# One decode step of an adaLN block: a row of w2 loaded in two parts over different DMA engines, five filler products fewer, one row of products cut finer

## The chip, the cores and the metric

The kernel runs on one core of one Trainium2 chip. The metric is the device time of one execution in microseconds (us); less is better. The core has five engines with queues of their own: PE (TensorE, matrix products), DVE (VectorE), ACT (ScalarE), POOL (GpSimd) and SP (SyncE, which here only issues loads). Sixteen DMA engines move the data between memory and the chip; one load is cut into shares that some or all of the sixteen carry, each engine working off its own list in order.

## The reference

Two tokens (B = 2, one position each, D = 512) pass through an attention block over a window of cached keys and values and then a feed-forward block, both with scales, shifts and gates computed from a condition `c`:

```
mod = silu(c) @ w_mod                              # six vectors of 512: sa, ca, ga, sb, cb, gb
h = layernorm(x) * (1 + ca) + sa
q = h @ wq                                         # 32 heads of 128
p = softmax(q . k / sqrt(128)) over the last 4096 of 32768 keys; o = p . v   # 8 kv heads
x = x + ga * (o @ wo)                              # wo: 4096 x 512
h = layernorm(x) * (1 + cb) + sb
x = x + gb * (silu(h @ w1) @ w2)                   # w1: 512 x 1792, w2: 1792 x 512
```

All is float32. The weights and the cache windows are 97.5 MB, and each byte is used for two tokens only.

## The kernel before, in words

All large inputs are loaded by SP, in the order in which they are used, into a ring of eight slots of 16 KB for each partition (`stream`, `load_group`, `load_runs`): w_mod, wq, then keys and values of four groups in turn, then wo, w1 and w2. A load waits on SP until its slot's last reader, on PE, is done. PE works off the products in the order of the program (`inorder`). A float32 product of the program stands in the profile as two records.

The end of the kernel is what the change touches. In the order of PE's queue:

- `busy(4)`: four filler products into a bank that nobody reads (`junk`, line 387). Each is a product of a 128x32 identity with a 128x512 tile of zeros.
- `acc_o` (line 417): 32 products with wo, four at a time in the four column groups of PE.
- `gather` (lines 396 to 410): ACT copies `acc_o` out of PSUM in two halves, and four small products (`ao`, line 404) add the four column groups up. Ahead of these four stands one filler product (`fill=1`), behind them another (`busy(1)`).
- DVE forms the new x and its column sums; `mean_b` (line 446) is a small product for the mean, and `busy(1)` follows it.
- `hid` (line 459): 16 products with w1, with the small product `var_b` (line 468) in the middle, and `busy(2)` behind them.
- DVE and ACT: transpose (`hidT`), scale (`z`), silu, to `uT` (line 487).
- w2 is 14 rows of 128 partitions x 512 numbers (`w2t[0]` to `w2t[13]`), in five loads: rows 0 to 7, rows 8 to 10, and rows 11, 12 and 13 alone. Rows 0 to 10 are the wide products `acc_yw` (line 491): row tt goes to column group tt % 4. ACT copies `acc_yw` to `y_sb` in two halves (line 513).
- `turned_products` (line 503): rows 11, 12 and 13 are multiplied the other way round, with the weights of w2 as the stationary side and two columns of `uT` moving. Between them the two halves of `y_sb` are turned and added in the same bank, `yx`. Row 11 goes in calls of 64 columns (`m=64`), the others in calls of 32.
- One scan on DVE (line 524) applies the gate, and ACT issues the store.

The host hands w2 over in another order of its columns, and takes the answer out of the stored tile.

Of the kernel before, what the change touches and what calls it, by code (L numbers as in the profile page):

```python
# [13 lines left out]
P = 128  # L14
B, D = 2, 512
HQ, HKV, DH = 32, 8, 128
G = HQ // HKV
F = 1792
# [5 lines left out]
def adaln_block(  # L24
# [21 lines left out]
    nc = tc.nc  # L46
# [12 lines left out]
    def const(shape, name):  # L59
        return consts.tile(shape, F32, name=name)  # L60

    def bank(tag, name):
        return (psum1 if tag in "CO" else psum).tile([P, 512], F32, tag=tag, name=name)
# [4 lines left out]
    def stream(n=1):  # L68
        i = turn_of[0]
        if n % 4 == 0:  # L70
            i += -i % n
        turn_of[0] = i + n
        return slots[:, i % RING : i % RING + n, :].rearrange("p s e -> p (s e)")
# [7 lines left out]
    def load_runs(w, per, lo, hi):  # L81

        e = w.shape[1]
        n = -(-(hi - lo) * e // 4096)
        t = stream(n)[:, : (hi - lo) * e].rearrange("p (q e) -> p q e", e=e)
        nc.sync.dma_start(t, w.rearrange("(p q) e -> p q e", q=per)[:, lo:hi, :])
        return t
# [104 lines left out]
    for k in range(4):  # L192
        ab = wm[:, k, : 2 * D].rearrange("p (s g m) -> p g s m", s=2, g=4)
        cd = wm[:, k, 2 * D :].rearrange("p (s g m) -> p g s m", s=4, g=4)
        for g in range(4):
            r = slice(32 * g, 32 * g + 32)
            nc.tensor.matmul(m_a[r, :], scT[:, k, :], ab[:, g], start=(k == 0), stop=(k == 3))  # L197
        for g in range(4):
            r = slice(32 * g, 32 * g + 32)
# [19 lines left out]
    hT, uT = const([P, 4, 32], "hT_b"), const([P, F // P, 32], "uT")  # L219
# [9 lines left out]
    for n in range(2):  # L229
        q_ps = bank("D", f"q{n}")  # L230
        for k in range(4):
            for g in range(4):
                lo = (16 * n + 4 * g) * DH
# [4 lines left out]
                    start=(k == 0),  # L238
                    stop=(k == 3),
# [3 lines left out]
        for g in range(G):  # L243
# [4 lines left out]
                start=True,  # L248
                stop=True,
            ))  # L250
        for b in range(B):
            for s in range(2):
                lo = 256 * (2 * b + n) + 48 * s
# [124 lines left out]
    for lo, hi in ((0, 3), (3, 4)):  # L378
        wt = load_runs(w1, 4, lo, hi)
# [4 lines left out]
    def busy(n):  # L384

        for _ in range(n):
            inorder(nc.tensor.matmul(  # L387
                junk[0:32, :],
                id4,
                warm,  # L390
                start=True,
                stop=True,
            ))


    def gather(acc, wide, name, start, stop, fill=0):

        sb_ = once.tile([P, D], F32, tag="wide", name=name)
        for c in (slice(0, D // 2), slice(D // 2, D)):
            inorder(nc.scalar.copy(sb_[:, c], wide[:, c]))  # L400
        if fill:
            busy(fill)
        for g in range(4):
            inorder(nc.tensor.matmul(
                acc[32 * g : 32 * g + 32, :],
                id4,
                sb_[:, g * P : (g + 1) * P],
                start=start,
                stop=stop,
            ))  # L410

    acc = bank("D", "acc_o")
    ao = bank("A", "ao")[:, :P]
    busy(4)
    for q in range(32):
# [5 lines left out]
            start=(q < 4),  # L421
            stop=(q >= 28),
        ))
    gather(ao, acc, "acc_o_sb", True, True, fill=1)
    busy(1)
    T2, WIDE = F // P, 11
    w2t = {}
    for lo, hi in ((0, 8), (8, 11), (11, 12), (12, 13), (13, T2)):
        wt = load_runs(w2, T2, lo, hi)
        for tt in range(lo, hi):  # L430
            w2t[tt] = wt[:, tt - lo, :]
    aoT = once.tile([P, 4, 32], F32, tag="zp", name="aoT")
# [11 lines left out]
    nc.vector.tensor_reduce(ks, x1T.rearrange("p k b -> p b k"), axis=AX.X, op=ALU.add)  # L444
    mean = bank("B", "mean_b")
    inorder(nc.tensor.matmul(mean[:, :B], mean512, ks, start=True, stop=True))
    busy(1)
    dT = once.tile([P, 4, B], F32, tag="dT", name="dT")
    nc.vector.tensor_sub(dT, x1T, mean[:, None, :B].to_broadcast([P, 4, B]))
    nc.vector.tensor_mul(hT[:, :, 0:32:16], dT, cbT[:, :, 0:32:16])  # L450
# [6 lines left out]
    for k in range(4):  # L457
        for g in range(4):
# [4 lines left out]
                start=(k == 0),  # L463
                stop=(k == 3),
            ))
        if k == 1:
# [3 lines left out]
            nc.scalar.activation(std, var[:, :B], AF.Sqrt, bias=eps_t)  # L470
            rstd = once.tile([P, B], F32, tag="rstdb", name="rstd_b")
            nc.vector.reciprocal(rstd, std)
    busy(2)
    hidT = once.tile([P, T2, 32], F32, tag="pr", name="hidT")
    nc.vector.transpose(hidT, hp.rearrange("p (m t) -> p t m", t=T2))
    z = once.tile([P, T2, B], F32, tag="z", name="z")
# [12 lines left out]
    for tt in range(WIDE):  # L489
# [5 lines left out]
            start=(tt < 4),  # L495
            stop=(tt >= WIDE - 4),
        ))

    def turned_products(rows, u, ks=range(4), start=False, stop=False, m=32):

        for k in ks:
            for g in range(0, P, m):
                inorder(nc.tensor.matmul(  # L503
                    yT[g : g + m, k, :, 0],
                    rows[:, k * P + g : k * P + g + m],
                    u,
                    start=start and k == 0,
                    stop=stop and k == 3,
                ))
# [2 lines left out]
    for c in (slice(0, D // 2), slice(D // 2, D)):  # L512
        inorder(nc.scalar.copy(y_sb[:, c], yw[:, c]))
    for h, tt in enumerate(range(WIDE, T2)):
        turned_products(
            w2t[tt],
            uT[:, tt, 0:32:16],
            start=(h == 0),
            stop=(tt == T2 - 1),
            m=32 if h else 64,  # L520
        )
        if h < 2:
            turned_products(y_sb, id4[:, 0:32:16], range(2 * h, 2 * h + 2))
    inorder(nc.vector.tensor_tensor_scan(yo, g0, yx, 0.0, op0=ALU.mult, op1=ALU.add))  # L524
# [48 lines left out]
```

## Time and profile before

| | |
|---|---|
| median of 3 runs | 233.94 us (233.76 to 233.95) |
| profiled execution | 233.89 us, of which 232.3 us are the profile's span |
| busy share of the span | PE 54%, weight loads 18%, DVE 9%, ACT 7%, POOL 2% |
| DMA | 97.66 MB at 420 GB/s over the span; 97.6% of the sixteen engines' time |
| mean granted clock of PE | 0.801 of full |

The profile covers one execution, from the first instruction to the end of the store. Rows of its views give the start, the time, the engine, the line of the program, the operation and the tiles (written <- read), with what ended the idle time before it in square brackets. PEld is the loading of a product's stationary side, which runs beside the products. The granted clock is what share of full speed the chip let PE run at; it is 1.00 or 0.50 in each stretch. The time of a product in the records holds its way through the array, so that products in a row overlap.

### The profile page before, as it was taken

The page shows a single profiled execution, that of the slowest core. Times are in us where ns is not written, and L with a number is a line of the kernel's source. Part 1 is how long each engine was busy: PE and PEld are TensorE (multiplying, and loading weights), DVE is VectorE, ACT ScalarE, POOL GpSimd, SP SyncE. Part 2 cuts the span into 40 slices and gives each one's busy share as a digit, 9 for nine tenths or more (in the row PEclk, how much of TensorE's full clock was granted, in tenths as well). Part 3 has the DMA queues.
Part 4 walks back from the last instruction along what each step waited for, and adds up shares of the span by engine and source line. Part 5 has one row for each costly group of instructions (what it writes and reads, how often), then busy time and mean ns, then how long its engine had stood idle before and what let it go on. Part 6 is the DMA issues. An engine that isn't in the chain of part 4 may idle for free.

```text
span 232.3 us, 2204 instructions
## 1 busy us (share of the span) xinstructions
PE 125.5 (54%) x976; PEld 42.4 (18%) x976; DVE 21.9 (9%) x74; ACT 17.3 (7%) x39; POOL 5.2 (2%) x22
## 2 busy tenths in 40 slices
PE   0004905840950781495096068139509506999877
PEld 0001401320210221121033012112202102232223
DVE  0005330110021000003000001200000210000230
ACT  2000210000012010001001000100100100000331
POOL 4003010000000000000000000000000000000000
PEclk9999995985796596578579659957857965999999
DMA  7999898998989989899899999999999999999993
GB/s 271 432 495 429 372 530 361 508 398 361 530 372 508 395 364 519 384 496 398 374 496 406 496 395 386 474 418 474 406 395 465 429 446 406 432 392 444 414 410 133
DMA packets 2916, 97.66 MB, mean 420 GB/s; under 512 B 460, under 2 KB 476, under 8 KB 1116
## 3 DMA queue, kind: packets, MB, share of 16 engines
q1 hardware_dynamic: 2748, 97.52, 97.6%
q8 instruction: 7, 0.11, 0.2%
q10 hardware_dynamic: 160, 0.01, 0.0%
q14 instruction: 1, 0.01, 0.0%
HBM read 97.53 MB, written 0.01 MB: 420 GB/s over the span
## 4 chain that ended last, share of the span: by engine, by line
DMA 76%; PE 22%; issue 1%; DVE 1%; SPq 0%
DMA slots<-in_A_v_cache_dram 50%; PE o L323 16%; DMA slots<-in_A_wq_dram 15%; DMA slots<-in_B_w_dram 10%; PE q L234 4%; PE acc_yw L491 1%; PE yx L503 1%; PE qT L244 0%; DVE q_sb L242 0%; SPq L102 0%; DVE xc L93 0%; DVE yo L524 0%
## 5 line engine op out<-in xcount | busy, mean ns | idle before, releaser
L272 PE MATMUL s<-slots,qs 128*32 128x512 f32 x256 | 36.6, 736 | 32.6 <-DMA slots<-in_A_k_cache_dram 32.6
L323 PE MATMUL o<-slots,probs 128*32 128x512 f32 x256 | 37.0, 739 | 25.5 <-DMA slots<-in_A_v_cache_dram 25.5
L323 PEld LDWEIGHTS o<-slots,probs 128*32 128x32 f32 x256 | 11.6, 129 | 47.7 <-issue 47.7
L272 PEld LDWEIGHTS s<-slots,qs 128*32 128x32 f32 x256 | 9.2, 132 | 56.7 <-issue 31.4
L197 PE MATMUL m_a<-slots,scT 128*32 128x256 f32 x32 | 4.0, 447 | 20.4 <-DVE scT L189 20.4
L234 PE MATMUL q<-slots,hq_T 128*32 128x512 f32 x64 | 8.9, 703 | 8.4 <-DMA slots<-in_A_wq_dram 8.4
L284 DVE TENSOR_REDUCE mx<-s 128x1 f32<-128x512 f32 x4 | 2.8, 692 | 68.1 <-PE s L272 68.1
L387 PE MATMUL junk<-warm,id 128*32 128x512 f32 x18 | 8.6, 595 | 0.3 <-DVE oTn L347 0.3
L336 ACT ACTIVATE ob<-o,rl 128x256 f32<-128x256 f32 x8 | 3.4, 470 | 64.7 <-PE o L323 64.7
L347 DVE COPY oTn<-oT 128x16 f32<-128x16 f32 x4 | 0.7, 185 | 67.9 <-PE oT L339 67.9
L417 PE MATMUL acc_o<-slots,oTn 128*32 128x512 f32 x64 | 7.1, 593 | 0.0
L200 PE MATMUL m_sp<-slots,scT 128*32 128x512 f32 x32 | 6.6, 712 | 0.0
L298 ACT COPY bias<-bp 128x1 f32<-128x1 f32 x4 | 0.6, 159 | 79.4 <-PE bp L294 79.4
L339 PE MATMUL oT<-id,ob 128*128 128x4 f32 x32 | 4.2, 255 | 2.3 <-ACT ob L336 2.3
L197 PEld LDWEIGHTS m_a<-slots,scT 128*32 128x32 f32 x32 | 1.1, 117 | 21.2 <-DVE scT L189 20.4
L339 PEld LDWEIGHTS oT<-id,ob 128*128 128x128 f32 x32 | 3.9, 191 | 5.9 <-ACT ob L336 5.9
L234 PEld LDWEIGHTS q<-slots,hq_T 128*32 128x32 f32 x64 | 2.3, 126 | 14.1 <-issue 14.1
L305 PE MATMUL lp<-rowsum,same 128*128 128x1 f32 x8 | 1.7, 282 | 5.6 <-ACT pr L300 3.2
L491 PE MATMUL acc_yw<-slots,uT 128*32 128x512 f32 x22 | 2.8, 599 | 1.6 <-DMA slots<-in_B_w_dram 1.6
L459 PE MATMUL hid<-slots,hT_b 128*32 128x448 f32 x32 | 3.4, 544 | 0.5 <-DMA slots<-in_B_w_dram 0.5
L303 DVE STREAM_TRANSPOSE probs<-pr 128x512 f32<-128x512 f32 x4 | 2.8, 711 | 7.2 <-ACT pr L300 7.2
L286 PE MATMUL mT<-ident,mx 128*1 128x128 f32 x8 | 1.5, 271 | 3.3 <-DVE mx L284 3.3
(108 smaller groups left out, 60.1 us busy)
## 6 DMA issues: line engine op xcount, KB each, us to landing
slots<-in_w_mod_dram SPq DMA_DIRECT2D x1, 6144.0 KB, 17.2
slots<-in_A_wo_dram SPq DMA_DIRECT2D x1, 6144.0 KB, 26.1
slots<-in_B_w_dram SPq DMA_DIRECT2D x1, 2688.0 KB
slots<-in_A_wo_dram SPq DMA_DIRECT2D x1, 2048.0 KB, 30.1
slots<-in_B_w_dram SPq DMA_DIRECT2D x1, 2048.0 KB
slots<-in_B_w_dram SPq DMA_DIRECT2D x1, 896.0 KB
slots<-in_B_w_dram SPq DMA_DIRECT2D x1, 768.0 KB
slots<-in_B_w_dram SPq DMA_DIRECT2D x3, 256.0 KB, 16.1
```

The lines of the kernel that those rows point to most:

```text
L197: nc.tensor.matmul(m_a[r, :], scT[:, k, :], ab[:, g], start=(k == 0), stop=(k == 3))
L200: nc.tensor.matmul(m_sp[r, :], scT[:, k, :], cd[:, g], start=(k == 0), stop=(k == 3))
L234: inorder(nc.tensor.matmul(q_ps[32 * g : 32 * g + 32, :], hq_T[:, k, :], wqt[:, k, lo : lo + 4 * DH], start=(k == 0), stop=(k == 3),))
L272: inorder(nc.tensor.matmul(s_ps[32 * c : 32 * c + 32, :], stat(grp, v, s), kt[grp][:, lo : lo + 512], start=(s == 0 and v == 0), stop=(s = ...
L284: nc.vector.tensor_reduce(mx, s_ps, axis=AX.X, op=ALU.max)
L323: inorder(nc.tensor.matmul(o_ps[r : r + 32, :], probs[grp % 2][:, 32 * n + 16 * s : 32 * n + 16 * s + 32], vt[grp][:, lo : lo + 512], star ...
L336: nc.scalar.activation(o_sb[:, c], o_ps[:, c], AF.Copy, scale=rl)
L339: inorder(nc.tensor.matmul(cols[:, 4 * v : 4 * v + 4], o_sb[:, v * DH : (v + 1) * DH], id4[:, 4 * v : 4 * v + 4], start=True, stop=True,))
L387: inorder(nc.tensor.matmul(junk[0:32, :], id4, warm, start=True, stop=True,))
L417: inorder(nc.tensor.matmul(acc[32 * g : 32 * g + 32, :], oTn[:, q, :], wot[q], start=(q < 4), stop=(q >= 28),))
L459: inorder(nc.tensor.matmul(hp[32 * g : 32 * g + 32, :], hT[:, k, :], w1t[k][:, g * FC : (g + 1) * FC], start=(k == 0), stop=(k == 3),))
L491: inorder(nc.tensor.matmul(yw[32 * g : 32 * g + 32, :], uT[:, tt, :], w2t[tt], start=(tt < 4), stop=(tt >= WIDE - 4),))
```

## The change

Three edits:

1. Row 8 of w2 is taken out of the load of rows 8 to 10. Its first 48 partitions are one load, whose source is written with an outer dimension of 3 (three shares of 16 partitions); its other 80 partitions are a second load (80 = 16 shares of 5); rows 9 and 10 are a third. The host permutes the 48 partitions of row 8 to match.
2. The filler products behind `acc_o` go: `fill=1`, both `busy(1)` and `busy(2)`, five in all. `busy(4)` ahead of `acc_o` stays.
3. Row 11 goes in two halves: the first in calls of 32 columns, the second in calls of 64.

```diff
-    def gather(acc, wide, name, start, stop, fill=0):
+    def gather(acc, wide, name, start, stop):
...
-        if fill:
-            busy(fill)
...
-    gather(ao, acc, "acc_o_sb", True, True, fill=1)
-    busy(1)
+    gather(ao, acc, "acc_o_sb", True, True)
     T2, WIDE = F // P, 11
     w2t = {}
+    rows = w2.rearrange("(p q) e -> p q e", q=T2)
     for lo, hi in ((0, 8), (8, 11), (11, 12), (12, 13), (13, T2)):
-        wt = load_runs(w2, T2, lo, hi)
+        if lo == 8:
+            wt = stream()[:, : 3 * D].rearrange("p (q e) -> p q e", e=D)
+            nc.sync.dma_start(
+                wt[:48, 0, :], rows[:48, 8, :].rearrange("(r a) e -> a r e", a=3)
+            )
+            nc.sync.dma_start(wt[48:, 0, :], rows[48:, 8, :])
+            nc.sync.dma_start(wt[:, 1:, :], rows[:, 9:11, :])
+        else:
+            wt = load_runs(w2, T2, lo, hi)
...
     inorder(nc.tensor.matmul(mean[:, :B], mean512, ks, start=True, stop=True))
-    busy(1)
...
-    busy(2)
     hidT = once.tile([P, T2, 32], F32, tag="pr", name="hidT")
...
     for h, tt in enumerate(range(WIDE, T2)):
-        turned_products(
-            w2t[tt],
-            uT[:, tt, 0:32:16],
-            start=(h == 0),
-            stop=(tt == T2 - 1),
-            m=32 if h else 64,
-        )
+        for half in range(2):
+            turned_products(
+                w2t[tt],
+                uT[:, tt, 0:32:16],
+                range(2 * half, 2 * half + 2),
+                start=(h == 0),
+                stop=(tt == T2 - 1),
+                m=32 if h or half == 0 else 64,
+            )
```

PE's queue from the fillers ahead of wo to the first turned row, before (`junk` is a filler, x4 stands for four calls):

```order
40 L387 MATMUL junk<-warm,id_58 32x512 x4
41 L417 MATMUL acc_o<-slots,oTn 32x512 x32
42 L387 MATMUL junk<-warm,id_58 32x512
43 L404 MATMUL ao<-acc_o_sb,id_58 32x128 x4
44 L387 MATMUL junk<-warm,id_58 32x512
45 L446 MATMUL mean_b<-ks,mean_101 128x2
46 L387 MATMUL junk<-warm,id_58 32x512
47 L459 MATMUL hid<-slots,hT_b 32x448 x8
48 L468 MATMUL var_b<-vs,mean_101 128x2
49 L459 MATMUL hid<-slots,hT_b 32x448 x8
50 L387 MATMUL junk<-warm,id_58 32x512 x2
51 L491 MATMUL acc_yw<-slots,uT 32x512 x11
52 L503 MATMUL yx<-uT,slots 64x2 x8
```

The same place now:

```order
40 L387 MATMUL junk<-warm,id_58 32x512 x4
41 L415 MATMUL acc_o<-slots,oTn 32x512 x32
42 L402 MATMUL ao<-acc_o_sb,id_58 32x128 x4
43 L452 MATMUL mean_b<-ks,mean_101 128x2
44 L464 MATMUL hid<-slots,hT_b 32x448 x8
45 L473 MATMUL var_b<-vs,mean_101 128x2
46 L464 MATMUL hid<-slots,hT_b 32x448 x8
47 L495 MATMUL acc_yw<-slots,uT 32x512 x11
48 L507 MATMUL yx<-uT,slots 32x2 x8
49 L507 MATMUL yx<-uT,slots 64x2 x4
```

Nothing but the fillers is gone between `acc_o` and `acc_yw`, and the first turned row has twelve calls instead of eight.

SP's queue at its end, as a difference (names in brackets are what an issue waits for: DMAHW0, 1 and 7 are landings of earlier loads, PE is the last reader of the slot; the first line before the difference is rows 0 to 7):

```order
 L86 DMA slots<-in_B_w_dram 128x4096 [waits PE_49]
-L86 DMA slots<-in_B_w_dram 128x1536 [waits DMAHW7_49,PE_49]
-L86 DMA slots<-in_B_w_dram 128x512 [waits PE_49] x2
+L429 DMA slots<-in_B_w_dram 48x1x512 [waits DMAHW7_49,PE_49]
+L432 DMA slots<-in_B_w_dram 80x512
+L433 DMA slots<-in_B_w_dram 128x1024 [waits PE_49]
+L86 DMA slots<-in_B_w_dram 128x512 [waits PE_49]
 L86 DMA slots<-in_B_w_dram 128x512 [waits DMAHW0_49,PE_49]
```

One load has become three, and the last row's load, which stood behind these, now waits for the landing of w1's first load (DMAHW1) as well.

More of the change, by code (lines that the diff above doesn't have):

```diff
@@ L550 @@
         inputs[name] = a.reshape(4, P, 4 * w)
-    inputs["B_w2"] = inputs["B_w2"].reshape(F, P, 4).transpose(0, 2, 1).reshape(F, D)
+    w2 = inputs["B_w2"].reshape(F, P, 4).transpose(0, 2, 1).reshape(P, F // P, D).copy()
+    w2[:48, 8] = w2[:48, 8].reshape(3, 16, D).transpose(1, 0, 2).reshape(48, D)
+    inputs["B_w2"] = w2.reshape(F, D)
     inputs["A_wo"] = inputs["A_wo"].reshape(HQ, DH, D).transpose(1, 0, 2).reshape(HQ * DH, D)
```

## The prediction

> **What bounds the kernel now.** I read the chain of work that ended last first, then the end of it in order of time, then the stretches of the granted clock. The chain's last rows (start, time, what):
>
> ```profile
> 202.77 23.34 DMA slots<-in_B_w_dram
> 226.25 2.81 PE acc_yw L491 x22
> 229.06 1.56 PE yx L503 x92
> 230.64 0.19 DVE yo L524
> ```
>
> The loads bound the kernel up to 226.1 us. From then on PE works without a pause to the last scan. So a microsecond is won by an earlier landing of w2's rows 0 to 7, which nothing here touches, or behind it on PE. The same place in order of time:
>
> ```profile
> 225.16 0.21 DVE L487 TENSOR_TENSOR uT<-z,sgh 128x28 f32<-128x28 f32 x1
> 226.25 2.81 PE L491 MATMUL acc_yw<-slots,uT 128*32 128x512 f32 x22 [1.64 <-DMA slots<-in_B_w_dram]
> 227.11 0.16 PEld L491 LDWEIGHTS acc_yw<-slots,uT 128*32 128x32 f32 x4 [0.27 <-issue]
> 228.00 0.15 PEld L491 LDWEIGHTS acc_yw<-slots,uT 128*32 128x32 f32 x6 [0.73 <-DMA slots<-in_B_w_dram]
> 228.99 0.55 PEld L503 LDWEIGHTS yx<-uT,slots 128*64 128x64 f32 x16 [0.84 <-issue]
> 229.18 0.65 ACT L513 COPY y_sb<-acc_yw 128x256 f32<-128x256 f32 x2 [4.63 <-PE acc_yw L491]
> 229.72 0.36 PEld L503 LDWEIGHTS yx<-uT,slots 128*32 128x32 f32 x31
> ```
>
> uT is ready at 225.37, 0.9 us before rows 0 to 7 are there: that is the slack of everything between wo and w2.
>
> **The change: row 8.** How even the DMA engines end is seen in the DMA share, the column before the last, of short stretches:
>
> ```profile
> 227.30:227.60 0.30, 0.30 (x11) 0.00 (x0) 0.00 (x0) 0.00 (x0) 0.00 (x0) 1.00 1.03 396
> 227.90:228.20 0.30, 0.30 (x7) 0.15 (x6) 0.00 (x0) 0.00 (x0) 0.00 (x0) 1.00 0.51 191
> 228.60:228.90 0.30, 0.30 (x6) 0.00 (x0) 0.00 (x0) 0.00 (x0) 0.00 (x0) 1.00 0.38 143
> 229.50:229.90 0.40, 0.40 (x42) 0.34 (x41) 0.00 (x0) 0.32 (x2) 0.00 (x0) 1.00 0.15 41
> ...
> q1 hardware_dynamic: 2748, 97.52, 97.6%
> L86 SPq DMA_DIRECT2D slots<-in_B_w_dram x7: 327/328/425, 201.0 to 214.3; - x7
> ```
>
> At 228 half of the sixteen have nothing left, and a few work on to almost 229.9. The queue's row gives one engine's pace: 97.52 MB in 97.6% of 16 x 232.3 us is 26.9 GB/s. Rows 8 to 10 are 48 KB an engine, 1.83 us. After the change every engine carries 10 KB (80 partitions of row 8) and 32 KB (rows 9, 10), 1.60 us, and three carry 32 KB more, 1.22 us: thirteen end 0.23 us earlier, three 0.99 us later. What two more completions cost an engine no row shows; between nothing and the 0.23 us they could eat, I take nothing, as 5 KB shares run at the pace of the rest.
>
> What it is worth: PE's groups of four in rows 0 to 7 stand 0.43 us apart (226.25, then the third at 227.11), so the fourth starts at 227.54 and PE is free at 227.97; the six weight loads of rows 8 to 10 came at 228.00. An earlier landing brings 0.03 us, no more. Rows 11 to 13 stand behind ACT's copies, which follow from the same products. So -0.03 us if the three are among the early half (their 0.99 us ends before 229.0, under the last engines' 229.8). If one of the three is among the last, row 8 lands 0.99 us late and PE with it: +0.96. No row names an engine. The early half is larger, so I take -0.03 and keep +0.96 for the range. The Trainium skill (DMA: Bandwidth & Descriptors, the section on why a DMA increments its semaphore by 16, "How many engines (k)") says that a load takes the lowest-numbered k engines, here numbers 0 to 2; no run here shows whether these end early.
>
> SP issues two loads more, 0.33 to 0.43 us each, and the last row's load now waits for w1's first load, whose landing let hid start at 219.25 (below). It is issued at about 219.2 instead of 214.3, and is needed by 230: the queue ahead of it covers it. Without that cover it would be short by what exceeds 10 us. PE's one wait for rows 8 to 10 becomes waits for three loads on one queue: a few hundredths, hidden under the fourth group. Zero for all of these.
>
> **The finer row 11.** Sixteen 64-wide weight loads take 0.55 us, 34 ns each; 31 32-wide ones 0.36, 12 ns each. Now 16 x 12 and 8 x 34 ns, 0.46 us: 0.09 less, but the next products wait for ACT's first copy, which ends at 229.55. Zero; without this cover -0.09.
>
> **The five fillers.** Ten of 18 records. What stands around them on PE:
>
> ```profile
> 214.53 0.61 PE L417 MATMUL acc_o<-slots,oTn 128*32 128x512 f32 x4
> 214.96 1.02 PE L387 MATMUL junk<-warm,id 128*32 128x512 f32 x2
> 215.70 0.57 PE L404 MATMUL ao<-acc_o_sb,id 128*32 128x128 f32 x6
> 216.10 0.28 PE L404 MATMUL ao<-acc_o_sb,id 128*32 128x128 f32 x2
> 217.41 0.38 PE L446 MATMUL mean_b<-ks,mean 128*128 128x2 f32 x2 [0.35 <-DVE ks L444]
> 219.25 1.71 PE L459 MATMUL hid<-slots,hT_b 128*32 128x448 f32 x16 [0.48 <-DMA slots<-in_B_w_dram]
> 222.73 1.88 PE L387 MATMUL junk<-warm,id 128*32 128x512 f32 x4
> ```
>
> Nobody reads them, and each gap that they fill ends by a wait for another engine or a load: taken alone they save nothing. But they are what keeps PE busy between 215.1 and 219.2 and from 222.9 to 226.2. The granted clock (third number from the end), in stretches of 3.41 us, the grid on which it changes; the first number behind the comma is PE's busy time:
>
> ```profile
> 85.04:88.46 3.42, 2.38 (x22) 1.16 (x12) 0.18 (x1) 0.84 (x2) 0.00 (x0) 1.00 1.06 460
> 88.46:91.87 3.41, 0.00 (x0) 0.00 (x0) 0.00 (x0) 0.00 (x0) 0.00 (x0) 0.50 0.75 327
> 95.28:98.70 3.42, 2.40 (x12) 0.60 (x16) 0.00 (x0) 0.00 (x0) 0.00 (x0) 0.50 0.80 345
> 98.70:102.11 3.41, 3.41 (x20) 0.79 (x16) 0.00 (x0) 0.00 (x0) 0.00 (x0) 0.50 1.24 538
> 102.11:105.52 3.41, 3.41 (x36) 0.96 (x32) 0.00 (x0) 0.00 (x0) 0.00 (x0) 1.00 0.89 384
> 105.52:108.94 3.42, 1.47 (x12) 0.38 (x4) 1.18 (x3) 0.44 (x2) 0.00 (x0) 1.00 0.82 350
> 108.94:112.35 3.41, 0.59 (x2) 0.50 (x2) 0.81 (x2) 0.50 (x2) 0.00 (x0) 0.50 1.21 521
> 143.07:146.48 3.41, 1.97 (x19) 0.46 (x12) 1.18 (x3) 0.00 (x0) 0.00 (x0) 1.00 0.98 423
> 146.48:149.90 3.42, 0.63 (x4) 0.46 (x4) 0.76 (x2) 0.94 (x3) 0.00 (x0) 1.00 0.84 364
> 149.90:153.31 3.41, 0.00 (x0) 0.00 (x0) 0.00 (x0) 0.00 (x0) 0.00 (x0) 0.50 1.20 519
> 214.76:218.17 3.41, 3.06 (x19) 0.97 (x15) 1.13 (x7) 1.61 (x4) 0.00 (x0) 1.00 0.95 406
> ```
>
> At full clock a stretch with 2.38 or 1.47 us of PE is followed by one at half; 1.97 us is the least here that was not. At half clock 2.40 us do not bring it back, a full stretch does. At half, 16 weight loads of wide products go where 32 go at full: PE's time doubles.
>
> Without the fillers the stretch from 214.76 holds acc_o to 215.14, ao (0.68) and mean_b (0.38), 1.44 us: less than 1.47. The clock falls at 218.17. hid, 219.25 to 222.73, is 3.48 us of work; at half clock until 225.00 (its first stretch holds 2.3 us, its second is full) 2.87 of it are done, the rest at full: 225.61, 2.88 late. uT follows at 228.25, past the landing: its 0.9 us of slack are spent, and acc_yw starts at 228.28 instead of 226.25. The stretch from 225.00 has 0.9 us of PE, so half clock again from 228.41. Rows 0 to 10 (226.25 to 228.99, 2.70 of work) do 0.13 to there, 1.70 by 231.82, 0.87 at full: 232.69, which is +3.70. The row-8 landing then gates nothing. Sum 233.89 + 3.70 = 237.6.
>
> That is for the grid of this one execution. If the grid lies 1.0 us later (boundaries 215.76, 219.17, 222.58): half from 219.17, back at 222.58, hid 1.66 late, acc_yw from 227.06, the next stretch at the limit with 1.98: +0.8, 234.7. If 2.2 later (216.96, 220.37, 223.78, 227.19): 1.5 us in the stretch before 220.37, hid 1.71 late, 0.9 us before 227.19, half through rows 0 to 7: +2.5, 236.4. I take the middle, 236.4; the case's own range is 234.6 to 237.7. The profiled execution lies 0.05 under the median of the runs, so nothing is added.
>
> **The rivals.**
> Not slower: the clock holds. Its place is the stretch with ao and mean_b, its price all of the 2.5 us, and it decides from the point where 1.44 us of PE, or what the chip counts in them, keeps full clock. For it: 2.38 us fell and 1.97 held, so busy time is not exactly what counts. Against: all rows under 1.97 fell. Time 233.89 - 0.03 = 233.86. The Trainium skill (TensorE: Matmul & The Clock Gate, "Why this matters for your kernels") gives one wholly idle window of about 3.4 us as what takes the clock back; by that rule it holds, as the longest gap left is 222.9 to 226.25. The rows from 85.04 and 105.52 disagree with it.
> A late engine: the clock holds, but one of row 8's three is among the last. +0.96 on PE's rows 8 to 10, 234.8; half that if it is one in the middle (0.38 of the sixteen at 228.7), 234.3.
> That the 48 partitions run over all sixteen after all would be the first rival's time.
>
> **How the numbers follow.** A change under 0.2%, 0.47 us, can hardly be told here. The clock falls 0.62 (of it 0.04 within 0.2%, where the grid is kind); it holds and row 8 is hidden 0.24 (0.20 within, 0.04 faster, should covers matter that I set to zero); it holds with a late engine 0.10 (0.07 slower, 0.03 within); others 0.04 (0.02 faster, 0.02 within). That is 0.65 slower, 0.29 the same, 0.06 faster. The range goes from just under the first rival to the traced grid's: 233.8 to 237.7.
>
> **What would show it.** Right: a granted clock of 0.50 in stretches behind 216 us, hid in about 2 times 3.5 us, uT after 227, acc_yw waiting for DVE and not for a load. Row 8: the DMA share at 228 higher, near 0.6, and gone before 229.8. Wrong: 1.00 to the end, uT again at 225.4 and acc_yw at 226.25; a late engine would stand as a longer wait of acc_yw's row 8 for its load than 0.03 us.

## The result and the profile after

The change makes the kernel slower: 236.51 us median of 5 runs (236.16 to 237.16) against 233.94 us of before (5 runs, 233.76 to 234.09), a ratio of 1.0115 (95% interval 1.0101 to 1.0130). The profiled execution took 236.16 us, of which 234.6 are the span, at a mean granted clock of 0.787 (before 233.89, 232.3 and 0.801). What follows compares the two spans, which differ by 2.3 us.

The main rows at the end of the chain of work that ended last (start, time, what):

```profile
201.94 24.80 DMA slots<-in_B_w_dram
226.75 0.14 issue
226.88 3.54 PE acc_yw L495 x17
...
230.72 0.66 PE acc_yw L495 x3
...
231.88 1.02 PE yx L507 x75
...
232.92 0.19 DVE yo L530
```

The loads still hand over to `acc_yw`, 0.63 us later than before (226.88 against 226.25). `acc_yw`, which took 2.8 us, now takes 4.5, and the scan starts at 232.92 instead of 230.64. From the start of `acc_yw` to the scan it is 6.04 us against 4.39: 1.65 more. So 0.63 + 1.65 = 2.28 us, the whole difference of the spans.

The row between loads and `acc_yw` in the chain of before:

```profile
226.12 0.14 issue
```

The end in order of time, five rows of it:

```profile
218.96 2.03 PE L464 MATMUL hid<-slots,hT_b 128*32 128x448 f32 x16 [1.48 <-DMA slots<-in_B_w_dram]
221.44 2.77 PE L464 MATMUL hid<-slots,hT_b 128*32 128x448 f32 x16
224.29 0.65 DVE L479 STREAM_TRANSPOSE hidT<-hid 128x448 f32<-128x448 f32 x1 [2.28 <-PE hid L464]
226.45 0.20 DVE L491 TENSOR_TENSOR uT<-z,sgh 128x28 f32<-128x28 f32 x1
226.88 4.04 PE L495 MATMUL acc_yw<-slots,uT 128*32 128x512 f32 x19 [2.67 <-DMA slots<-in_B_w_dram]
```

The second half of `hid` takes 2.77 us, as its products take at half clock, and `uT` is ready at 226.65 instead of 225.37. But `acc_yw` waits for a load: rows 0 to 7 land at 226.75 (the last share of their load) instead of 226.12. Two things are late by the same moment.

Stretches on this execution's own grid of clock changes; behind the stretch and its length stand the busy times of PE, PEld, DVE, ACT and POOL, then the granted clock, the DMA share and GB/s:

```profile
213.39:216.80 3.41, 2.14 (x24) 0.56 (x16) 0.62 (x3) 0.65 (x2) 0.00 (x0) 1.00 0.96 414
216.80:220.22 3.42, 1.65 (x18) 0.79 (x18) 0.77 (x6) 1.45 (x2) 0.00 (x0) 1.00 1.01 426
220.22:223.63 3.41, 3.41 (x22) 1.10 (x18) 0.17 (x1) 1.54 (x2) 0.00 (x0) 0.50 1.04 444
223.63:227.04 3.41, 0.74 (x12) 0.19 (x8) 1.94 (x7) 0.23 (x1) 0.00 (x0) 1.00 0.96 289
227.04:230.46 3.42, 3.42 (x21) 1.07 (x16) 0.00 (x0) 0.00 (x0) 0.00 (x0) 0.50 0.65 249
```

The clock is halved in two stretches, the one with `hid` and the one with `acc_yw`. Each follows on a stretch in which PE has little to do (1.65 and 0.74 us). The row 223.63:227.04 has a second message, which the forecast did not have: 289 GB/s at a DMA share of 0.96. The engines are nearly all busy and move a third less than in the row above it. The stretches at the very end, as shown of before:

```profile
227.90:228.20 0.30, 0.30 (x4) 0.00 (x0) 0.00 (x0) 0.00 (x0) 0.00 (x0) 0.50 0.87 335
228.60:228.90 0.30, 0.30 (x8) 0.09 (x3) 0.00 (x0) 0.00 (x0) 0.00 (x0) 0.50 0.71 273
229.50:229.90 0.40, 0.40 (x7) 0.03 (x2) 0.00 (x0) 0.00 (x0) 0.00 (x0) 0.50 0.30 113
```

Before, the share here was 0.51, 0.38 and 0.15. In the trace the first share of the last row lands at 228.46 instead of 227.98, and the last share at 230.27 instead of 229.83: the engines are all behind, not three of them.

### The profile page after: what moved, and what is told of

The parts are those of the page before. It is cut to its first block, busy times and chain, and to the rows that moved or that the text cites. A ratio compares the mean times of both kernels' runs of the same rounds, so it can differ in the third digit from the quotient of the medians.

```text
span 234.6 us, 2204 instructions
## 1 busy us (share of the span) xinstructions
PE 126.9 (54%) x974; PEld 43.7 (19%) x974; DVE 22.0 (9%) x74; ACT 17.3 (7%) x39; POOL 5.2 (2%) x22
## 4 chain that ended last, share of the span: by engine, by line
DMA 75%; PE 22%; issue 1%; DVE 0%; SPq 0%; ACT 0%; ACTq 0%
DMA slots<-in_A_v_cache_dram 49%; PE o L323 15%; DMA slots<-in_A_wq_dram 15%; DMA slots<-in_B_w_dram 11%; PE q L234 4%; PE acc_yw L495 2%; PE yx L507 0%; PE qT L244 0%; SPq L102 0%; DVE q_sb L242 0%; ACT y_sb L517 0%; DVE xc L93 0%; DVE yo L530 0%; ACTq L517 0%
## 5 line engine op out<-in xcount | busy, mean ns | idle before, releaser
L272 PE MATMUL s<-slots,qs 128*32 128x512 f32 x256 | 37.2, 746 | 32.2 <-DMA slots<-in_A_k_cache_dram 32.2
L323 PE MATMUL o<-slots,probs 128*32 128x512 f32 x256 | 36.2, 725 | 24.2 <-DMA slots<-in_A_v_cache_dram 24.2
L234 PE MATMUL q<-slots,hq_T 128*32 128x512 f32 x64 | 9.9, 779 | 7.3 <-DMA slots<-in_A_wq_dram 7.3
L200 PE MATMUL m_sp<-slots,scT 128*32 128x512 f32 x32 | 7.2, 732 | 0.0
L495 PE MATMUL acc_yw<-slots,uT 128*32 128x512 f32 x22 | 4.5, 931 | 2.7 <-DMA slots<-in_B_w_dram 2.7
L464 PE MATMUL hid<-slots,hT_b 128*32 128x448 f32 x32 | 4.8, 726 | 1.5 <-DMA slots<-in_B_w_dram 1.5
L387 PE MATMUL junk<-warm,id 128*32 128x512 f32 x8 | 3.6, 595 | 0.3 <-DVE oTn L347 0.3
L415 PEld LDWEIGHTS acc_o<-slots,oTn 128*32 128x32 f32 x64 | 2.4, 109 | 5.1 <-issue 4.7
```

The costliest lines, as they stand in the source:

```text
L200: nc.tensor.matmul(m_sp[r, :], scT[:, k, :], cd[:, g], start=(k == 0), stop=(k == 3))
L234: inorder(nc.tensor.matmul(q_ps[32 * g : 32 * g + 32, :], hq_T[:, k, :], wqt[:, k, lo : lo + 4 * DH], start=(k == 0), stop=(k == 3),))
L272: inorder(nc.tensor.matmul(s_ps[32 * c : 32 * c + 32, :], stat(grp, v, s), kt[grp][:, lo : lo + 512], start=(s == 0 and v == 0), stop=(s = ...
L323: inorder(nc.tensor.matmul(o_ps[r : r + 32, :], probs[grp % 2][:, 32 * n + 16 * s : 32 * n + 16 * s + 32], vt[grp][:, lo : lo + 512], star ...
L387: inorder(nc.tensor.matmul(junk[0:32, :], id4, warm, start=True, stop=True,))
L415: inorder(nc.tensor.matmul(acc[32 * g : 32 * g + 32, :], oTn[:, q, :], wot[q], start=(q < 4), stop=(q >= 28),))
```

## The experiments

The theory after the result: the missing fillers let the clock fall (the forecast's reason). The rival: the split of row 8 delays all of w2, and the fall of the clock is its consequence or comes beside it. The third edit stood as costless. Times are given against the runs of before on the same chip (medians 233.72, 233.84 and 233.86 in the three groups); the ratio's 95% interval is in brackets. Because the clock's grid lies elsewhere in each execution, runs of one kernel scatter more here than those of before do.

### Each edit alone, and the fillers put back

**Edit 1 alone** (e1_row8): before, with row 8 of w2 in two loads.

```diff
+        if lo == 8:
+            ...
+            nc.sync.dma_start(wt[:48, 0, :], rows[:48, 8, :].rearrange("(r a) e -> a r e", a=3))
+            nc.sync.dma_start(wt[48:, 0, :], rows[48:, 8, :])
+            nc.sync.dma_start(wt[:, 1:, :], rows[:, 9:11, :])
```

> Before with the first edit alone: row 8 of w2 in two loads, the first over three DMA engines; all fillers kept. The prediction's own step: 0.03 us less than before, 233.9. Theory of the shared pace (from the trace of the changed kernel, where the DMA engines moved 300 GB/s between 224 and 226.2 us at a share of 1.00, against 391 at 0.94 before): the three-engine load slows all sixteen, rows 0 to 7 land 0.6 us later, PE starts acc_yw at 226.85 instead of 226.25, and the time is 234.5. Granted clock 1.00 behind 198 us under both.

Measured: 236.30 us (6 runs), ratio 1.0089 [1.0065, 1.0114]. The runs fall in two groups: 234.73 and 234.96, and four of 236.30 to 236.49. The profiled one is of the first group (span 233.3), with all of its end at full clock. From its timeline:

```profile
227.28 2.77 PE L500 MATMUL acc_yw<-slots,uT 128*32 128x512 f32 x22 [2.84 <-DMA slots<-in_B_w_dram]
231.14 0.42 PE L512 MATMUL yx<-uT,slots 128*32 128x2 f32 x30
```

`acc_yw` takes its old 2.77 us, but starts at 227.28, 1.03 us later than before, because rows 0 to 7 land at 227.14. So the split alone costs 1.0 us at full clock (the spans), and 2.6 us in the four runs of the second group, of which there is no trace; a trace of e6_row8_run, below, shows the clock falling in such a run. These rows stand ahead of row 8 in the queue, and `uT` was ready at 225.18. The forecast's -0.03 us is wrong.

**Edit 2 alone** (e2_fillers): before, without the five fillers.

```diff
-    gather(ao, acc, "acc_o_sb", True, True, fill=1)
-    busy(1)
+    gather(ao, acc, "acc_o_sb", True, True)
...
-    busy(1)
...
-    busy(2)
```

> Before with the second edit alone: the five fillers behind acc_o gone, loads and row 11 as before. Clock theory: granted clock 0.50 in one or two stretches behind 216 us, hid 1.7 to 2.9 us late, time 234.7 to 237.6, near 236.4. If instead the new loads made the changed kernel slow: 233.9, clock 1.00 to the end.

Measured: 236.02 us (8 runs, 234.29 to 237.62), ratio 1.0092 [1.0059, 1.0126]. The profiled execution (236.11):

```profile
219.09 2.36 PE L457 MATMUL hid<-slots,hT_b 128*32 128x448 f32 x16 [1.52 <-DMA slots<-in_B_w_dram]
226.58 0.20 DVE L484 TENSOR_TENSOR uT<-z,sgh 128x28 f32<-128x28 f32 x1
226.84 4.45 PE L488 MATMUL acc_yw<-slots,uT 128*32 128x512 f32 x22 [2.50 <-DVE uT L484]
```

Here the chain is the one forecast: `hid` slow, `uT` at 226.78, and `acc_yw` waits for DVE; rows 0 to 7 had landed at 225.94. The products of `acc_yw` then take 4.45 us at half clock. The fillers alone are enough for a loss of the size seen.

**Edit 3 alone** (e3_fine): before, with row 11 in two halves, the first in calls of 32.

```diff
-        turned_products(w2t[tt], uT[:, tt, 0:32:16], ..., m=32 if h else 64)
+        for half in range(2):
+            turned_products(w2t[tt], uT[:, tt, 0:32:16], range(2 * half, 2 * half + 2),
+                ..., m=32 if h or half == 0 else 64)
```

> Before with the third edit alone: the first half of row 11 in calls of 32 columns, 16 records more on PE. Prediction's step: 0.0 us, since the next products wait for ACT's first copy anyway; 233.9. Rival: the extra records shift the instruction fetch of the end onto a DMA engine that still carries w2, then the last landing is 0.5 to 1.4 us later and the time up to 235.

Measured: 235.67 us (6 runs, 233.74 to 236.05), ratio 1.0069 [1.0043, 1.0096]; five of six runs lie at 235.2 to 236.1. The profiled one (235.42) has full clock until 231.76. Its end:

```profile
230.08 0.41 PE L503 MATMUL yx<-uT,slots 128*32 128x2 f32 x29
231.93 0.13 PEld L503 LDWEIGHTS yx<-uT,slots 128*32 128x32 f32 x1 [1.53 <-issue]
231.93 0.21 PE L503 MATMUL yx<-uT,slots 128*32 128x2 f32 x1 [1.45 <-issue]
232.18 0.19 DVE L526 TENSOR_TENSOR_SCAN yo<-g,yx 128x16 f32<-128x16 f32 x1 [6.89 <-PE yx L503]
```

All of the kernel is as before up to the last weight load and product, which come 1.5 us late and wait for nothing that the profile shows ("issue"). A scan that stood at 230.64 starts at 232.18. The edit adds 16 records to PE's program (1991 in the trace against 1975).

**Edits 1 and 3, fillers back** (e4_refill): the changed kernel with all five fillers.

```diff
-    gather(ao, acc, "acc_o_sb", True, True)
+    gather(ao, acc, "acc_o_sb", True, True, fill=1)
+    busy(1)
...
+    busy(1)
...
+    busy(2)
```

> The changed kernel with the five fillers put back (edits one and three alone). Clock theory alone: back to 233.9. Clock and shared pace of the three-engine load: 234.5, with clock 1.00 and acc_yw from 226.8. If the fillers had nothing to do with it: 236.5.

Measured: 236.33 us (4 runs, 236.18 to 236.91), ratio 1.0107 [1.0093, 1.0122]: the loss of the changed kernel, with its fillers in place. Timeline and stretches of the profiled execution:

```profile
227.71 3.54 PE L500 MATMUL acc_yw<-slots,uT 128*32 128x512 f32 x19 [3.03 <-DMA slots<-in_B_w_dram]
```

```profile
225.30:228.71 3.41, 1.00 (x12) 0.49 (x16) 0.12 (x1) 0.00 (x0) 0.00 (x0) 1.00 0.97 302
228.71:232.13 3.42, 3.42 (x34) 1.11 (x25) 0.00 (x0) 0.00 (x0) 0.00 (x0) 0.50 0.25 91
```

The late landing (227.57) makes PE idle for 3.03 us, the stretch has 1.00 us of work, and the clock falls behind it with `busy(2)` in place. So late loads bring the fall of the clock with all fillers there. This kernel has the finer row 11 too; e6_row8_run, below, shows the same without it.

### The split: what makes the loads slow

In four kernels one thing was varied at a time, all with the fillers and the old row 11.

**48 partitions over all sixteen engines** (e5_row8_16), so nothing is concentrated on three:

```diff
-            nc.sync.dma_start(wt[:48, 0, :], rows[:48, 8, :].rearrange("(r a) e -> a r e", a=3))
+            nc.sync.dma_start(wt[:48, 0, :], rows[:48, 8, :])
```

> Before with row 8 in the same two loads of 48 and 80 partitions, but the 48 over all sixteen DMA engines, three partitions each (no outer dimension of 3, no permutation on the host). If the concentration on three engines slows all sixteen: the pace stays, rows 0 to 7 land at 226.1 and the time is 233.7 to 233.8. If it is the number of loads or the small 2 KB pieces: rows 0 to 7 land about 1 us late as in e1, 234.7 to 236.3.

**Consecutive rows at the source** (e6_row8_run), so the three shares read memory in runs:

```diff
-                wt[:48, 0, :], rows[:48, 8, :].rearrange("(r a) e -> a r e", a=3)
+                wt[:48, 0, :], rows[:48, 8, :].rearrange("(a r) e -> a r e", a=3)
```

> The first edit with three engines as before, but each engine's 16 partitions are consecutive in memory too (engine a reads rows 16a to 16a+15 of the 48 instead of rows a, a+3, ...; no permutation on the host). If the interleaved reading is what slows the pace: rows 0 to 7 land at 226.1 and 233.8. If it is three engines with 16 partitions each: rows 0 to 7 about 1 us late, 234.7 to 236.3 as in e1.

**The last 48 partitions instead of the first** (e7_row8_hi):

```diff
-                wt[:48, 0, :], rows[:48, 8, :].rearrange("(r a) e -> a r e", a=3)
+                wt[80:, 0, :], rows[80:, 8, :].rearrange("(a r) e -> a r e", a=3)
...
-            nc.sync.dma_start(wt[48:, 0, :], rows[48:, 8, :])
+            nc.sync.dma_start(wt[:80, 0, :], rows[:80, 8, :])
```

> As the run before, but the three engines carry the last 48 partitions (80 to 127) and the sixteen carry the first 80. If the slow pace comes from the memory side or from any three engines writing in a bunch: 234.7 to 236.3. If it comes from which partitions the three write: rows 0 to 7 at 226.1 and 233.8, or another delay than e6's.

**Rows 8, 9 and 10 in one load each, 128 partitions** (e9_single): as many loads and as short pieces as with the split, and no share cut otherwise.

```diff
-    for lo, hi in ((0, 8), (8, 11), (11, 12), (12, 13), (13, T2)):
+    for lo, hi in ((0, 8), (8, 9), (9, 10), (10, 11), (11, 12), (12, 13), (13, T2)):
```

> Before with rows 8, 9 and 10 of w2 in one load each, all 128 partitions, eight a DMA engine as in all other loads: as many loads and as small pieces (2 KB) as in the first edit, but no engine carries other partitions than usual. If loads of fewer than 128 partitions, which give the engines other partitions than the rest of the queue, slow the pace: 437 GB/s or near it between 224 and 227 us as before, rows 0 to 7 landed at 226.1, 233.8. If it is the number of loads or the 2 KB pieces: 300 GB/s, rows 0 to 7 about 0.8 us late, 234.8.

| run | median us (range) | ratio [95%] | rows 0 to 7 landed, profiled |
|---|---|---|---|
| e5_row8_16 | 234.87 (234.84 to 234.93) | 1.0046 [1.0034, 1.0059] | 226.88 |
| e6_row8_run | 236.43 (234.79 to 236.87) | 1.0100 [1.0074, 1.0126] | 226.97 |
| e7_row8_hi | 235.83 (235.29 to 236.73) | 1.0098 [1.0078, 1.0118] | 226.86 |
| e9_single | 245.47 (245.17 to 246.04) | 1.0501 [1.0484, 1.0517] | 226.34 |

Four runs each. The time of e9_single says nothing on the question: its two loads more take two slots more of the ring, so its last two loads go into slots that hold w1, `hid` waits for them until 229.8 and multiplies rows of w2 there. What it does show is the pace of its loads up to then; the kernel before, whose pace between 224 and 226 us is the measure, moves 387 GB/s there and not the 437 of the expectation. The stretch from 224 to 226 us in seven kernels, the last two columns being DMA share and GB/s; first before:

```profile
224.00:226.00 2.00, 0.61 (x2) 0.00 (x0) 0.97 (x5) 0.23 (x1) 0.00 (x0) 1.00 0.92 387
```

The changed kernel, and e1_row8:

```profile
224.00:226.00 2.00, 0.21 (x4) 0.00 (x0) 1.35 (x5) 0.23 (x1) 0.00 (x0) 1.00 1.01 307
```

```profile
224.00:226.00 2.00, 0.44 (x2) 0.00 (x0) 0.82 (x4) 0.23 (x1) 0.00 (x0) 1.00 1.00 285
```

e5_row8_16, e6_row8_run and e7_row8_hi, in this order:

```profile
224.00:226.00 2.00, 0.45 (x2) 0.00 (x0) 0.83 (x4) 0.23 (x1) 0.00 (x0) 1.00 1.00 304
```

```profile
224.00:226.00 2.00, 0.52 (x2) 0.00 (x0) 0.89 (x4) 0.23 (x1) 0.00 (x0) 1.00 1.01 318
```

```profile
224.00:226.00 2.00, 0.55 (x2) 0.00 (x0) 0.90 (x5) 0.23 (x1) 0.00 (x0) 1.00 0.97 308
```

And e9_single:

```profile
224.00:226.00 2.00, 0.00 (x0) 0.00 (x0) 0.00 (x0) 0.00 (x0) 0.00 (x0) 0.50 0.97 389
```

In each kernel with row 8 cut at partition 48 or 80, the engines are busy nearly all the time and move 285 to 318 GB/s; without the cut they move 387 and 389 at 0.92 and 0.97. It is not the three engines (e5 has none and is as slow), not the order in which memory is read (e6), not which partitions (e7), and not the number of loads or pieces of 2 KB (e9). One more difference of e9_single is that rows 9 and 10 are not one load there, as they are in the five slow kernels (pieces of 4 KB). The trace of the changed kernel speaks against that rival, ahead of the last landing of row 8 (227.29) and behind it:

```profile
226.40:226.80 0.40, 0.00 (x0) 0.00 (x0) 0.22 (x2) 0.00 (x0) 0.00 (x0) 1.00 0.98 261
227.30:227.80 0.50, 0.50 (x8) 0.24 (x4) 0.00 (x0) 0.00 (x0) 0.00 (x0) 0.50 0.99 393
```

In the second stretch rows 9 and 10 are still being loaded (to 228.43), row 8 is not, and the pace is back. What the slow kernels share is that an engine's share of row 8 covers other partitions than its 8 of the rest of the queue, so that engines work on different pieces of the same partitions. That is the difference that remains, and it is not shown to be the cause: no run cut row 8 into loads that keep the 8 partitions of each engine. Where in the chip it costs is open.

The late landing is only the first part of the price. In the traces of e6_row8_run and e7_row8_hi, both with all fillers and the old row 11, the stretch of the clock's grid into which the landing falls and the one behind it are, first e6:

```profile
224.57:227.98 3.41, 0.88 (x9) 0.36 (x13) 0.62 (x3) 0.00 (x0) 0.00 (x0) 1.00 0.99 301
227.98:231.39 3.41, 3.41 (x18) 0.79 (x10) 0.00 (x0) 0.00 (x0) 0.00 (x0) 0.50 0.40 151
```

```profile
225.00:228.41 3.41, 1.42 (x16) 0.61 (x17) 0.26 (x2) 0.00 (x0) 0.00 (x0) 1.00 0.99 291
228.41:231.82 3.41, 3.41 (x126) 1.70 (x117) 0.00 (x0) 0.65 (x2) 0.00 (x0) 1.00 0.39 135
```

In e6_row8_run PE waits for the late rows, has 0.88 us of work, and the clock falls: 236.38 us. In e7_row8_hi the grid lies 0.43 us later, 1.42 us of work fall into the stretch, and the clock stays: 235.43 us. So the split alone can cost all that the whole change costs.

### The finer row: what makes the last pair late

**One filler fewer far ahead** (e10_fine_b3): e3_fine with `busy(3)` for `busy(4)`, ahead of `acc_o`. **One filler fewer at `busy(2)`** (e8_fine_m1): e3_fine with `busy(1)`. Both take 4 records out of PE's program.

```diff
-    busy(4)
+    busy(3)
```

> Row 11 finer as in e3, and one filler of busy(4) ahead of acc_o fewer (4 records), so that the fillers behind acc_o, which keep the clock, all stay. Theory of the instruction block: the program ends before the new block, no stall at the end, 233.8 with clock 1.00. If the finer calls are slow by themselves or if any filler counts for the clock: 235.2 to 236 as in e3 and e8.

```diff
-    busy(2)
+    busy(1)
```

> The third edit (row 11 finer, 16 records more) with one filler of busy(2) fewer (4 records fewer). In e3 the last pair of PE's records came 1.5 us late with nothing to wait for. Theory of the instruction block: these two records were the first of a new 16 KB block of PE's program that was still being fetched; with 4 records fewer the program ends before it and the stall goes: 233.7, clock 1.00. Rival, that finer calls themselves stall PE at the end: 235.4 to 236.0 again.

Measured: e10_fine_b3 234.35 us (11 runs, 233.94 to 234.84), ratio 1.0023 [1.0014, 1.0031]. Its end:

```profile
230.19 0.42 PE L503 MATMUL yx<-uT,slots 128*32 128x2 f32 x30
230.68 0.19 DVE L526 TENSOR_TENSOR_SCAN yo<-g,yx 128x16 f32<-128x16 f32 x1 [5.34 <-PE yx L503]
```

The last pair is in time, with the same finer row, so the finer products alone do not make the pause. What fits is a border in PE's program, past which the code is not there yet: in e3_fine the last pair lies past it, and with 4 records fewer it lies ahead of it. That is inferred; the views show no fetch. The 16 KB packet of the instruction queue at 229.61 in the trace of e3_fine is no sign of it, because kernels without the pause have one too (229.67 before, 229.58 in e10_fine_b3).

Two more traces bear on it. The runs of e10_fine_b3 are still 0.5 us behind before (0.3 in the span), though the scan starts at 230.68 against 230.64. The rest stands behind the scan: one of PE's closing instructions, which the views leave out, starts 0.72 us after the one ahead of it in the trace, against 0.15 before. It stands four records further on in the program than the first late record of e3_fine, which is what a border at a fixed place of the program gives. And e4_refill, with the same products on PE as e3_fine, shows no pause in its last row of products:

```profile
233.18 0.45 PE L512 MATMUL yx<-uT,slots 128*32 128x2 f32 x30
```

PE gets there 3 us later than in e3_fine. So the length of the program alone is not enough; PE must apparently also come to the border early. One of the six runs of e3_fine (233.74) has no loss either.

e8_fine_m1 has no pause either, but 235.39 us (6 runs, 234.27 to 235.65), ratio 1.0062 [1.0047, 1.0077]:

```profile
223.28:226.69 3.41, 1.14 (x10) 0.34 (x12) 1.71 (x7) 0.23 (x1) 0.00 (x0) 1.00 0.94 391
226.69:230.11 3.42, 3.42 (x23) 1.04 (x15) 0.00 (x0) 0.00 (x0) 0.00 (x0) 0.50 0.52 199
```

One filler of the two ahead of `acc_yw` is enough to lose the full clock behind it: 1.14 us of PE in the stretch, with the old loads and all other fillers there.

### The changed kernel without the split, and the first three fillers alone

**Edits 2 and 3 without edit 1** (e11_nosplit): the changed kernel with row 8 back in the load of rows 8 to 10.

```diff
-        if lo == 8:
-            ...
-        else:
-            wt = load_runs(w2, T2, lo, hi)
+        wt = load_runs(w2, T2, lo, hi)
```

> The changed kernel with rows 8 to 10 in one load again (edits two and three alone). Clock theory: as e2, spread by where the clock's grid falls, 234.3 to 237.6, median near 236.0; the changed kernel's own 236.5 would then owe the split 0.5 or less, although the split alone costs 1 to 2.6. If the split and the fillers add up: 234.5 to 235.5.

Measured: 237.48 us (4 runs, 236.97 to 237.57), ratio 1.0149 [1.0135, 1.0163]: not better than the changed kernel, but worse. (The grid lies elsewhere too, so this is no gain of the split.) Stretches of the profiled execution (237.57); the one between the second and third row is at half clock too:

```profile
215.00:218.41 3.41, 1.34 (x14) 0.58 (x10) 1.23 (x7) 1.71 (x4) 0.00 (x0) 1.00 0.96 408
218.41:221.83 3.42, 2.52 (x16) 0.68 (x16) 0.17 (x2) 0.39 (x1) 0.00 (x0) 0.50 1.06 450
...
225.24:228.65 3.41, 0.91 (x12) 0.16 (x8) 1.94 (x7) 0.23 (x1) 0.00 (x0) 1.00 0.84 331
228.65:232.06 3.41, 3.41 (x21) 0.86 (x16) 0.00 (x0) 0.00 (x0) 0.00 (x0) 0.50 0.08 28
```

The clock falls at 218.41, ahead of `hid`, stays low to 225.24, and falls again at 228.65. `uT` is ready at 228.23 and `acc_yw` starts at 228.28. This is the forecast's case for the traced grid, which had 218.17, 225.00 and 228.41 for the clock, so a grid 0.24 us earlier, and 228.25, 228.28 and 237.6 us for the rest.

**The three fillers ahead of `hid` away, `busy(2)` kept** (e12_nofirst), with the old loads and the old row 11.

```diff
-    gather(ao, acc, "acc_o_sb", True, True, fill=1)
-    busy(1)
+    gather(ao, acc, "acc_o_sb", True, True)
...
     inorder(nc.tensor.matmul(mean[:, :B], mean512, ks, start=True, stop=True))
-    busy(1)
```

> Before without the three fillers between acc_o and hid; the two behind hid stay. Clock theory: the clock falls ahead of hid where the grid puts a stretch into the gap (about 6 in 10 positions), and stays otherwise: runs in two groups, 233.8 and 234.7 to 236.4. If only the gap behind hid matters: 233.8 in all.

Measured: 235.04 us (4 runs, 234.55 to 235.72), ratio 1.0051 [1.0031, 1.0071]. Stretches and timeline of the profiled execution (234.57):

```profile
215.55:218.97 3.42, 1.07 (x10) 0.59 (x10) 1.39 (x8) 2.02 (x4) 0.00 (x0) 1.00 0.93 394
218.97:222.38 3.41, 3.04 (x16) 0.68 (x16) 0.00 (x0) 0.07 (x1) 0.00 (x0) 0.50 1.09 465
222.38:225.80 3.42, 3.42 (x26) 1.16 (x22) 1.34 (x5) 1.54 (x2) 0.00 (x0) 1.00 0.94 399
```

```profile
226.98 2.77 PE L489 MATMUL acc_yw<-slots,uT 128*32 128x512 f32 x22 [0.80 <-DVE uT L485]
```

The first fall is there, `uT` comes at 226.93, and `acc_yw` starts 0.73 us late. But `busy(2)` fills the stretch from 222.38, and `acc_yw` runs its 2.77 us at full clock. So the three fillers are worth the first fall, and the two of `busy(2)` guard against the second. The group at 233.8 that the expectation had for the kinder places of the grid did not show in four runs. No kernel of these beats before.

## Why the prediction was right, and where not

The number came out (236.4 forecast, 236.51 measured), and so did the main step; two other steps did not, and the sum hides both. That the two figures lie 0.1 us apart is luck in part. The forecast took the middle of three places of the grid, and the profiled execution happened to have that one. And each half of the change gives nearly the same time by itself: 236.02 for the fillers (e2_fillers), 236.30 for the split (e1_row8), 236.33 for split and finer row (e4_refill).

- **The five fillers: right, in size and place.** The clock falls behind stretches with too little PE work, slows `hid`, delays `uT` and then halves the clock of `acc_yw`. The forecast's third grid (borders 220.37, 223.78, 227.19; +2.5 us) is within 0.2 us that of the profiled execution (220.22, 223.63, 227.04; +2.3 us). From the start of `hid` to `uT` it was 7.69 us against 6.12 before, 1.57 more where 1.71 was forecast; `hid` started 0.29 us earlier. Shown by e2_fillers, e11_nosplit and e12_nofirst, and for one filler alone by e8_fine_m1.
- **The grid as the main doubt: right.** e11_nosplit met the traced grid's case within 0.1 us on nearly the same grid, and the runs of e2_fillers (234.29 to 237.62) span nearly all of the case's own range (234.6 to 237.7).
- **Row 8, -0.03 us: wrong.** The step that failed is "5 KB shares run at the pace of the rest", and with it "three engines 0.99 us later, thirteen 0.23 earlier". The three shares landed between 226.04 and 226.48, ahead of the last of rows 0 to 7 at 226.75, so the three engines are early ones, as the step took them to be. The Trainium skill (DMA: Bandwidth & Descriptors, "How many engines (k)") puts such a load on the lowest-numbered engines; no row here names an engine, so whether these three are those is not shown. But all sixteen became slower. Measured alone the term is +1.0 us where the clock stays full (e1_row8's trace, e5_row8_16), about the bound of +0.96 kept for a late engine but for another reason, and +2.6 us where the clock falls behind the late landing (median of e1_row8, e6_row8_run).
- **"The row-8 landing then gates nothing": right of row 8, wrong of the loads.** Row 8 itself had landed at 227.29, and PE came to it at 229.27. But its split held up rows 0 to 7, and `acc_yw` waited for these (its row above), not for DVE as announced. Rows 0 to 7 landed at 226.75, and `uT` was ready at 226.65. Either alone makes `acc_yw` late (227.28 in e1_row8, 226.84 in e2_fillers), and undoing the split (e11_nosplit) or putting the fillers back (e4_refill) does not bring the time back. How much of the 2.3 us belongs to which edit therefore has no single answer.
- **The finer row 11, zero: right in the sum only.** Alone it costs 1.5 us in the profiled execution. In the changed kernel the 20 records that went with the fillers more than pay for the 16 added (1972 records against 1975 before), and the pause does not appear: the last `yx` runs without a gap up to the scan at 232.92. The step counted the time of the weight loads, and not what 16 records more do to the end of the program.
- **SP's two issues more, zero: not contradicted.** The first of them took SP 0.80 us and not 0.33 to 0.43, but SP had issued all three loads by 210.1, long before PE needs them. The last row landed at 230.27 instead of 229.83, with the late queue, and nothing waits long for it.
- **The rival "the clock holds": fell.** Stretches with 1.65, 1.34, 1.07, 1.14 and 0.74 us of PE work at full clock were followed by half clock, as the rows under 1.97 had said. But 1.97 is no threshold: 1.42 us kept the clock in e7_row8_hi, and 2.38 lost it in the forecast's own row from 85.04, so busy time is not exactly what counts. The Trainium skill (TensorE: Matmul & The Clock Gate, "Why this matters for your kernels") asks for no idle gaps of PE above about 3 us, one window of idle. By that the clock would have stayed: the longest idle time of PE at this place in the changed kernel was 2.67 us. The measurement decides against it here.
- **What would show it.** The halved stretches and `uT` after 227 as announced, but for 0.35 us; `hid` at half clock only from 220.22 on; the DMA share at 228 higher than 0.6 (0.87) and not gone before 229.8 (0.30 there), which is the sign of the row-8 step being wrong.

## What to carry to other kernels

Before a product that nobody reads is removed, add up the work that is left in each stretch of the clock's grid, at several places of the grid, and follow the delay to the next stretch: the second fall cost more than the first here. After a load is cut, compare the GB/s at a DMA share near 1 with that of before; a cut in which each engine keeps the partitions that it has in the rest of the queue is the one to try first, though no run here made it. Where one number comes out as forecast, still take each edit alone: here two causes were late by the same moment, and one of three edits was harmless beside another that had shortened the program.

## What was not expected of the hardware

- One row of 128 partitions cut into loads of 48 and 80 lowered the pace of all sixteen engines from 387 GB/s to between 285 and 318 at a DMA share of 0.97 to 1.01, also for the rows queued ahead of it (landed 0.6 to 1.5 us late). The same row as a load of 128 partitions kept 389 GB/s.
- 16 more records in PE's program made the last pair of them 1.5 us late (e3_fine); 4 fewer elsewhere brought it back in time (e10_fine_b3).
- No single amount of PE work in a stretch marks where the full clock is lost: 1.42 us kept it in e7_row8_hi, 1.65 us lost it in the changed kernel.
- The grid on which the clock changes lies elsewhere in each execution (a border at 216.80, 218.41, 218.97 and, before, 218.17), and the same five missing fillers cost 0.6 us in one run and 3.9 in another (e2_fillers, 234.29 and 237.62 against 233.72 of before). That the grid makes this spread is read from traces of single runs, and fits the forecast's cases.
